# Recurrent memory attention, backward chain: output gradient by head in four column groups, 32-bit sums in column groups, LayerNorm input by DMA

## The chip, the cores and the metric

The kernel runs on one core of one Trainium2 chip. The metric is the device time of one execution in microseconds (us). Five instruction queues work side by side: TensorE (PE, with its weight loads shown as PEld), VectorE (DVE), ScalarE (ACT), GpSimd (POOL) and SyncE (SP), which only issues DMAs. SP and POOL issue the DMAs of the stage told here; 16 DMA engines carry them out.

## The reference

A layer of attention over segments with a recurrent memory, then a gated feed-forward layer, and the gradients of all of it. With S = 2048 rows, D = 448 columns, H = 16 heads of Dh = 256 (HD = 4096), M = 8 memory rows, segments of 32 rows (64 of them), so L = 40 rows per attention:

```python
mem = mem0
for s in range(n_seg):
    h = concatenate([mem, xs[s]])                     # 8 + 32 = 40 rows of 448
    q, k, v = h @ Wq, h @ Wk, h @ Wv                  # 16 heads of 256
    p = softmax(where(mask, q @ k.T / 16, -1e9))      # 40 x 40 per head
    o = (p @ v) @ Wo                                  # 40 rows of 448
    mem, out[s] = o[:8], o[8:]
h  = x + attention(layernorm(x))
h2 = h + (silu(layernorm(h) @ w_gate) * (layernorm(h) @ w_up)) @ w_down
return h2, vjp(grad_out)                              # h2 and nine gradients
```

Each segment takes its memory from the one before it; backwards, each segment's output gradient needs the memory gradient of the segment after it. So the 64 segments are a chain in both directions.

## The kernel before

The kernel has four stages, one after the other: the forward chain (to about 940 us of the span), the feed-forward layer with its gradients (to about 1257 us), the backward chain (`backward_chain`, to about 2253 us), and a tail with the weight gradients. The change lies in the backward chain and in the PSUM pools that it takes.

The loop of the backward chain runs over the segments s = 63 to 0, with `t, r = divmod(s, 4)`: four segments make a tile of 128 rows, and a tile is worked in the order r = 3, 2, 1, 0. The instructions within `with k.prio.crit()` go in the order in which they are written ahead of everything else; others fill the gaps as the scheduler places them. DMAs started with `nc.sync` stand in SP's queue in order, those with `nc.gpsimd` in POOL's. Each DMA of SP takes one of eight semaphores in turn and is issued when the DMA that had it before has landed.

What one segment does, with the lines of the kernel before:

- `prep_tile` (L1147, at r = 2 for the next tile) loads 128 rows of the output gradient from the DRAM tensor `DHb`, turned, as one transposing DMA of 128 x 512; POOL copies them into `do_roll` (L1150). `do_roll` holds, per segment, 40 columns: 0 to 31 are the segment's rows, 32 to 39 its memory rows, which the segment just worked has left there. The kernel keeps this order of the 40 rows throughout.
- `load_seg` (L1155 to L1168) loads the values turned (`load_v`, L1153, a transposing DMA), eight pieces of the queries and keys (L1163, runs of 2048 bytes, from the DRAM tensors T and T0) and, on POOL, the probabilities `P_sb` (L1166), which POOL copies to block-diagonal form (L1168).
- Output gradient: `WoT` as weights, `do_roll` as the moving side, 128 matmuls of 40 columns (L1236), so that each head's gradient comes out turned (`doT`); 16 transposes (L1245) give the same by rows (`dO_sb`).
- Score gradients: 32 matmuls (L1254), four DVE operations (L1261 to L1267) to `dS_bd`.
- `heads` (L1213): value, key and query gradients, 16 matmuls each; of the 40 rows, 0 to 7 (`first_rows`) go to `lo`, and 8 to 39 (`own_rows`) to `blk`. The turning of `dS_bd` is L1304.
- `rows_in` (L1293): 3 x 32 matmuls of 448 columns into one PSUM bank `pH`, four at a time in four column groups of 32, that is, four partial sums lie in the four groups of 32 partitions.
- `om` (L1319) copies `pH`; four fp32 matmuls with the matrix `sel` as moving side (L1322) add the four partial sums and turn them; the last eight of the 32 rows go to `do_roll` as the next segment's memory gradient (L1326), the other 24 are staged for the LayerNorm input `dxT`.
- Once per tile, outside the critical order and so filling gaps: the same products for the `lo` rows (L1378), their sums (L1385), four transposes of `dxT` (L1393), the LayerNorm gradient (`ln_bwd`, L253 to L264), and the stores.

All PSUM tiles come from three rotating pools: five banks `ps`, two `fx`, one `po`.

Of the kernel before, what the change touches and what calls it, by code (L numbers as in the profile page):

```python
# [9 lines left out]
FP32 = mybir.dt.float32  # L10
# [5 lines left out]
P = 128  # L16
# [129 lines left out]
def run_all(k: _K):  # L146
# [15 lines left out]
    psum = ctx.enter_context(tc.tile_pool(name="psum", bufs=1, space=bass.MemoryType.PSUM))  # L162
# [41 lines left out]
    def dt(name, shape, dtype=BF16):  # L204
# [7 lines left out]
              X_o=dt("X_o", [NB, P, MC * P]), HC=dt("HC", [NB * P, DP]), Oh=dt("Oh", [S, D]),  # L212
              DC0=dt("DC0", [P, 4, D]), DC1=dt("DC1", [P, NB - 4, D]))
# [18 lines left out]
    ffn_phase(k, lambda: next(back, None))  # L232
    for _ in back:
        pass
# [874 lines left out]
def backward_chain(k: _K):  # L1109
# [7 lines left out]
    NWIN = 8  # L1117

    WoT_sb = W(0, KC, HD)
# [4 lines left out]
    lo_b = {"v": [A(40, 32, 32), A(42, 32, 32)], "k": [A(44, 32, 32), A(46, 32, 32)], "q": [B(5, 32, 32)]}  # L1124
    dxT = B(7, 1024).bitcast(FP32).rearrange("p (c n) -> p c n", n=P)
    vT = A(49.5, 16, 2 * L)
    dO_sb = A(52, 16, P)
    doT = A(56, 32, 64)
    do_roll = A(60, KC, NWIN, L)
    xn_t = B(9, D)  # L1130
    dh_h = [B(9.875, 448).bitcast(FP32), A(48.5, 448).bitcast(FP32)]
    dx3 = A(48, KC * 48).bitcast(FP32).rearrange("p (c n) -> p c n", c=KC)
    lq3 = k.mv2[:].rearrange("p t n -> p (t n)").bitcast(BF16).rearrange("p (c m) -> p c m", m=M)
    dx2 = [(A(64.5, 96).bitcast(FP32).rearrange("p (c n) -> p c n", c=2), 0, 2, P, 2),
           (A(48.375, 48).bitcast(FP32).rearrange("p (c n) -> p c n", c=1), 2, 3, P, 2),
           (k.maskb[:, 0:24].unsqueeze(1), 3, 4, 64, 2)]
    dx1 = B(4.375, KC * 48).bitcast(FP32).rearrange("p (c n) -> p c n", c=KC)
    dx_stage = [(dx3, 0, KC, P, 3)] + dx2 + [(dx1, 0, KC, P, 1)]
    dhx = A(62.5, KC, P)
    dmr = A(63.5, KC, 16, M)  # L1140
    P_bd, dS_bd, dST_bd = [B(1.25 * i, 8, 2, L) for i in range(3)]
    Pb = [B(3.75, 8, L)]

    def prep_tile(t):
        if t < 0:
            return
        nc.sync.dma_start_transpose(out=dhx, in_=dr["DHb"][t * P:(t + 1) * P, :])  # L1147
        s0 = (4 * t) % NWIN
        for kc in range(KC):
            nc.gpsimd.tensor_copy(out=do_roll[:, kc, s0:s0 + 4, 0:SEG], in_=dhx[:, kc, :].rearrange("p (g j) -> p g j", g=4))  # L1150
# [4 lines left out]
    def load_seg(s):  # L1155
        if s < NSEG - 1:
            load_v(s)
# [488 lines left out]
```

## Time and profile before

Times of three runs: 2938.78 us median (2931.57 to 2948.37). The profiled execution took 2921.87 us.

| what | value |
|---|---|
| profiled execution, its span | 2921.87 us, 2920.1 us |
| clock granted to TensorE, mean | 0.995 |
| TensorE busy in 0 to 940, 940 to 1257, 1257 to 2253, 2253 to 2920 us | 873.6, 306.0, 979.0, 647.3 us |
| mean busy share of the DMA engines in the same four | 0.75, 0.93, 0.55, 0.81 |
| DVE, ACT, POOL busy in 1257 to 2253 us | 516, 380, 233 us |
| packets of the hardware queue, of the software queue | 692788, 49872 |

How to read it: a busy share is an average over stages, so the stages are taken apart by windows. A matmul's row gives start, length, line, what it writes and reads, and how many of the kind follow each other; lengths overlap a little, so costs are taken from start to start. "Waits" give who stood idle for what. A DMA's row on SP is the time of its issue; the transfer lands later, and the page counts what it moved in packets.

### The profile page before, as it was taken

The page shows a single profiled execution, that of the slowest core. Times are in us where ns is not written, and L with a number is a line of the kernel's source. Part 1 is how long each engine was busy: PE and PEld are TensorE (multiplying, and loading weights), DVE is VectorE, ACT ScalarE, POOL GpSimd, SP SyncE. Part 2 cuts the span into 40 slices and gives each one's busy share as a digit, 9 for nine tenths or more (in the row PEclk, how much of TensorE's full clock was granted, in tenths as well). Part 3 has the DMA queues.
Part 4 walks back from the last instruction along what each step waited for, and adds up shares of the span by engine and source line. Part 5 has one row for each costly group of instructions (what it writes and reads, how often), then busy time and mean ns, then how long its engine had stood idle before and what let it go on. Part 6 is the DMA issues. An engine that isn't in the chain of part 4 may idle for free.

```text
span 2920.1 us, 108265 instructions
## 1 busy us (share of the span) xinstructions
PE 2805.9 (96%) x47650; PEld 1746.3 (60%) x47650; DVE 1328.6 (45%) x3320; ACT 1077.0 (37%) x2590; POOL 704.1 (24%) x1676
## 2 busy tenths in 40 slices
PE   4999999999999999989999999999999989999998
PEld 3555565555555555667777777677766544545444
DVE  4555565556455666745555555555554011111110
ACT  2554454455454454433333333343333011111110
POOL 1222232233222222422222222222222111212211
PEclk9999999999999999999999999999999999999999
DMA  7577777777778988985555555555555998969941
GB/s 258 152 193 192 192 193 195 192 194 200 198 185 229 285 219 215 257 259 151 142 145 154 144 141 155 137 148 149 142 154 170 347 269 175 207 183 238 207 147 52
DMA packets 743132, 552.14 MB, mean 189 GB/s; under 512 B 601796, under 2 KB 639060, under 8 KB 740100
## 3 DMA queue, kind: packets, MB, share of 16 engines
q1 hardware_dynamic: 692788, 402.38, 55.9%
q0 software_dynamic: 49872, 142.83, 14.4%
q8 instruction: 374, 6.13, 0.9%
q14 instruction: 98, 0.80, 0.1%
HBM read 169.84 MB, written 236.13 MB: 139 GB/s over the span
## 4 chain that ended last, share of the span: by engine, by line
PE 80%; issue 8%; DMA 4%; ACT 3%; DVE 2%; POOL 2%; SPq 0%; POOLq 0%; ACTq 0%; DVEq 0%
PE po L1293 11%; PE psf L1487 8%; PE psf L1236 7%; PE psf L569 6%; PE psf L704 5%; PE psf L1213 5%; PE psf L967 4%; PE po L751 4%; PE fx L1378 3%; PE fx L1487 3%; PE fx L1091 3%; PE psf L593 2%; PE psf L1322 2%; PE psf L1245 2%; PE psf L485 2%
## 5 line engine op out<-in xcount | busy, mean ns | idle before, releaser
L76 ACT CAST arA<-psf 128x384 bf16<-128x384 f32 (+6 forms) x1083 | 419.8, 428 | 845.0 <-PE psf L1487 215.1
L75 DVE CAST arA<-psf 128x256 bf16<-128x256 f32 (+6 forms) x797 | 358.4, 471 | 687.8 <-PE psf L1487 248.9
L1293 PE MATMUL po<-arW,arA 128*32 128x448 bf16 x6144 | 328.1, 355 | 5.6 <-DMA arW<-Tq 4.1
L1487 PEld LDWEIGHTS <-arA 128*128 128x128 bf16 x1440 | 139.0, 98 | 160.6 <-issue 4.8
L1236 PEld LDWEIGHTS <-arW 128*128 128x128 bf16 x8192 | 211.2, 96 | 23.3 <-issue 18.4
L1487 PE MATMUL psf<-arW,arA 128*128 128x512 bf16 x882 | 222.7, 381 | 0.0
L1293 PEld LDWEIGHTS <-arA 128*32 128x32 bf16 x6144 | 146.8, 96 | 120.3 <-ACT arA L76 9.3
L1236 PE MATMUL psf<-arA,arW 128*128 128x40 bf16 x8192 | 217.2, 180 | 0.8 <-DVE arA L1326 0.8
L704 PE MATMUL psf<-arW,arA 128*64 128x512 bf16 x1536 | 212.1, 382 | 0.0
L569 PE MATMUL psf<-arW,arA 128*32 128x512 bf16 x3072 | 189.8, 381 | 7.7 <-DVE arA L75 0.9
L76 ACT COPY arA<-psf 128x512 bf16<-128x512 bf16 (+3 forms) x206 | 142.9, 727 | 39.5 <-PE psf L593 24.0
L76 ACT CAST arB<-psf 128x64 bf16<-128x64 f32 (+1 forms) x320 | 107.7, 337 | 135.1 <-PE psf L576 73.6
L967 PE MATMUL psf<-arW 128*128 128x256 bf16 (+1 forms) x1288 | 149.0, 277 | 5.0 <-DVE arA L75 3.7
L75 DVE COPY arA<-psf 128x512 bf16<-128x512 bf16 (+2 forms) x204 | 104.3, 512 | 99.5 <-PE psf L1245 82.4
L967 PEld LDWEIGHTS <-arW 128*128 128x128 bf16 (+1 forms) x1344 | 103.2, 97 | 56.9 <-issue 45.4
L569 PEld LDWEIGHTS <-arA 128*32 128x32 bf16 x3072 | 70.3, 96 | 105.1 <-issue 28.8
L751 PE MATMUL po<-arW,arA 128*32 128x256 bf16 (+1 forms) x4096 | 126.9, 261 | 1.2 <-DVE arA L75 1.2
L1564 POOL DMA_DIRECT2D out_dram<-arA x96 | 52.2, 544 | 262.0 <-DVE arA L75 233.6
L1527 PE MATMUL psf<-arW 128*128 128x448 bf16 x525 | 111.6, 352 | 3.0 <-DVE arA L75 1.6
L1213 PEld LDWEIGHTS <-arW 128*128 128x128 bf16 x2048 | 79.5, 99 | 49.6 <-issue 48.1
L751 PEld LDWEIGHTS <-arA 128*32 128x32 bf16 x4096 | 104.0, 96 | 8.5 <-DVE arA L75 1.5
L1168 POOL COPY arB<-arB 40x320 bf16<-40x320 bf16 x128 | 58.9, 460 | 174.8 <-DMA arB<-P_all 86.7
(298 smaller groups left out, 4553.5 us busy)
## 6 DMA issues: line engine op xcount, KB each, us to landing
arW<-T SPq DMA_DIRECT2D x256, 128.0 KB
X_o<-arA SPq DMA_DIRECT2D x37, 512.0 KB
T<-arA SPq DMA_DIRECT2D x64, 256.0 KB
X_v<-arA POOLq DMA_DIRECT2D x30, 512.0 KB, 4.9
X_k<-arA POOLq DMA_DIRECT2D x30, 512.0 KB, 4.7
X_q<-arA POOLq DMA_DIRECT2D x30, 512.0 KB, 4.1
out_dram<-arA POOLq DMA_DIRECT2D x84, 128.0 KB, 3.8
VG<-arA SPq DMA_DIRECT2D x64, 160.0 KB
```

The lines of the kernel that those rows point to most:

```text
L75: return nc.vector.tensor_copy(out=out, in_=in_)
L76: return nc.scalar.copy(out=out, in_=in_)
L569: nc.tensor.matmul(banks[b][w][32 * q:32 * q + 32, :], lhsT=hT_roll[:, kc, sl, M:L], rhs=(Wq_sb, Wk_sb)[w][:, kc, col(q, b)], start=(b == ...
L704: nc.tensor.matmul(pV[b][64 * g:64 * g + 64, 0:512], lhsT=hT_flat[:, kc, sl * L:sl * L + 64], rhs=Wv_sb[:, kc, n * 512:(n + 1) * 512], sta ...
L751: last = nc.tensor.matmul(pO[32 * q:32 * q + 32, 0:w], lhsT=xblk[:, j, r * SEG:(r + 1) * SEG], rhs=Wo_sb[:, cj(j), 256 * dh:256 * dh + w], ...
L967: nc.tensor.matmul(ps[fp][:, f2 * 256:(f2 + 1) * 256], lhsT=Wt[lo:hi, kc, c * P:(c + 1) * P], rhs=xT[lo:hi, kc, :], start=(kc == 0 and f2 ...
L1091: k.last_dh = nc.tensor.matmul(pdh[:, 0:D], lhsT=srcT[:, tt, c, :], rhs=WT[:, c, :], start=(i == 0), stop=(i == 2 * FC - 1))
L1213: nc.tensor.matmul(ps[b][:, i * 2 * L:(i + 1) * 2 * L], lhsT=lhs[:, at, :], rhs=rhs_bd[:, cl // 2, :, :].rearrange("p g n -> p (g n)"), st ...
L1236: nc.tensor.matmul(pss[b][:, jj * L:(jj + 1) * L], lhsT=WoT_sb[:, kc, c * P:(c + 1) * P], rhs=do_roll[:, kc, sl, :], start=(kc == 0), stop ...
L1293: nc.tensor.matmul(pH[32 * (j % 4):32 * (j % 4) + 32, 0:D], lhsT=blk[nm][:, j, r * SEG:(r + 1) * SEG], rhs=WT[:, cj(j), :], start=(nm == " ...
L1487: k.last_mm = nc.tensor.matmul(pa[i][:, 0:w], lhsT=lhs_of(b)[:, i // 2 * P:(i // 2 + 1) * P], rhs=rhs_of(q, b, i % 2), start=(b == 0), sto ...
L1527: k.last_mm = nc.tensor.matmul(pa[i][:, 0:D], lhsT=lhs_of(b, i), rhs=rhs_of(b), start=(bi == 0), stop=(bi == m + 3))
```

## The change

The diff touches `backward_chain` and the PSUM pools:

- PSUM: after the feed-forward stage the three pools are closed, and eight banks are named one by one (`k.bank(i)`).
- Output gradient (`grads_by_col`): now columns 8 to 39 of `do_roll` (the "own" rows) are the weights and `WoT` the moving side, 512 columns wide, in four column groups (one per group of heads): 32 matmuls instead of 128. D = 448 is held as four chunks of 112. Eight transposes (`grads_turned`) give the turned form. Rows 0 to 7 (the "rest", which need no other segment) are done for the four segments of a tile at once (`hRo`), one tile ahead, at the ends of r = 2 and r = 1; they are saved to DRAM (`RO`) and loaded again by rows (`load_rest`).
- Value gradients: `value_rest` and `value_own`, 8 + 8 matmuls of 160 columns, with probabilities loaded by twelve small DMAs (`load_p`).
- Sums: `summed` has `sel` as weights, and adds the four partial sums by four fp32 matmuls of 112 columns, in column groups; the result is cast (`ot`), turned by one transpose and copied to `do_roll`.
- LayerNorm input: the summed rows go to DRAM (`DXQ` per segment, `DXR` per tile) and are loaded as a tile of 128 x 448 (`norm_load`); `norm_first` and `norm_second` replace `ln_bwd` here, two tiles later. The products of the `lo` rows are issued by hand (`rest_parts`) in numbers per segment.
- `prep_tile` is called at r = 3 and loads 112-column chunks of `DHb`, four transposing calls of 128 x 112. In the order of the built program the four stand as plain copies with a pattern 112 x 128 x 1, where the one of before stands as a transpose.

The loads of a segment stand in SP's queue in the order `load_rest`, `load_p`, `load_v`, `load_qk`, DXQ, DXR, norm loads (r = 2), `prep_tile` (r = 3).

```diff
+    k.bank = bank
+    k.ps1 = lambda: turns("ps", 0, 5, "psf")
+    k.fx1 = lambda: turns("fx", 5, 2, "fx")
+    k.po1 = lambda: bank(7, "po")
+    k.ph1 = lambda: psum2.tile([P, 1024], BF16, tag="bank7", name="ph", bufs=1)
...
     def prep_tile(t):
         if t < 0:
             return
-        nc.sync.dma_start_transpose(out=dhx, in_=dr["DHb"][t * P:(t + 1) * P, :])
+        for c in range(4):
+            nc.sync.dma_start_transpose(out=dhx[0:DQ, c, :], in_=dr["DHb"][t * P:(t + 1) * P, DQ * c:DQ * c + DQ])
         s0 = (4 * t) % NWIN
-        for kc in range(KC):
-            nc.gpsimd.tensor_copy(out=do_roll[:, kc, s0:s0 + 4, 0:SEG], in_=dhx[:, kc, :].rearrange("p (g j) -> p g j", g=4))
+        for c in range(4):
+            nc.gpsimd.tensor_copy(out=do_roll[0:DQ, c, s0:s0 + 4, 0:SEG], in_=dhx[0:DQ, c, :].rearrange("p (g j) -> p g j", g=4))
+        nc.gpsimd.tensor_copy(out=hRo[0:DQ].rearrange("p k (g j) -> p k g j", j=M), in_=do_roll[0:DQ, :, s0:s0 + 4, 0:M])
+
+    def grads_by_col(lhs, bank, b, c0=0, c1=4):
+        for c in range(c0, c1):
+            for q in range(4):
+                n0 = 1024 * q + 512 * b
+                last = nc.tensor.matmul(bank[32 * q:32 * q + 32, :], lhsT=lhs(c), rhs=WoT_sb[0:DQ, c, n0:n0 + 512],
+                                        start=(c == 0), stop=(c == 3), skip_group_check=True)
+        return last
+
+    def rest_lhs(c):
+        return hRo[0:DQ, c, :]
+
+    def grads_turned(bank, src, dst, b, eng="v"):
+        pt = bank[:].bitcast(BF16)
+        for i in range(4):
+            last = nc.tensor.transpose(pt[:, i * P:(i + 1) * P], src[:, i * P:(i + 1) * P], ident[:, :])
+        return last, k.evac(dst.rearrange("p (x c) n -> p x c n", x=2)[:, :, 8 * b:8 * b + 8, :],
+                            pt[:, 0:512].rearrange("p (c x n) -> p x c n", x=2, n=32), eng)
+
+    def rest_saved(t, b, src):
+        nc.sync.dma_start(out=dr["RO"][t][:, 512 * b:512 * b + 512], in_=src)
+
+    def load_rest(s):
+        t, r = divmod(s, 4)
+        src = dr["RO"][t].rearrange("(q r k) n -> r q k n", q=4, k=M)
+        for w, a, m, n in ((0, 0, 0, 3), (1, 0, 3, 3), (0, 3, 6, 2)):
+            nc.sync.dma_start(out=dOr[32 * w:32 * w + 32, a:a + n].rearrange("p m e -> p (m e)"), in_=src[r][:, :, P * m:P * (m + n)])
+
+    def load_p(s):
+        pa = dr["P_all"][s].rearrange("p (x i n) -> p x i n", x=2, n=L)
+        for q in range(4):
+            g, x = divmod(q, 2)
+            for w in range(2):
+                p0 = 32 * w + M * q
+                nc.sync.dma_start(out=P4r[p0:p0 + M, 2 * x + g], in_=pa[64 * g:64 * g + M, x])
+            nc.sync.dma_start(out=P4[32 * q:32 * q + 32, 2 * x + g], in_=pa[64 * g + M:64 * g + L, x])
...
+    def value_rest(ps):
+        for m in (0, 3, 1, 4, 2, 5, 6, 7):
+            w, a = divmod(m, 3) if m < 6 else (0, m - 3)
+            last = nc.tensor.matmul(v_out(ps, m), lhsT=dOr[32 * w:32 * w + 32, a, :], rhs=p_rows(P4r[32 * w:32 * w + 32], m),
+                                    start=m in (0, 3, 6), stop=False, skip_group_check=True)
+        return last
+
+    def value_own(ps, m0, m1):
+        for m in range(m0, m1):
+            last = nc.tensor.matmul(v_out(ps, m), lhsT=dO_own[:, m * P:(m + 1) * P], rhs=p_rows(P4, m),
+                                    start=False, stop=True, skip_group_check=True)
+        return last
...
+    def summed(ps, part):
+        for q in range(4):
+            last = nc.tensor.matmul(ps[32 * q:32 * q + 32, 0:DQ], lhsT=sel[:], rhs=part[:, DQ * q:DQ * q + DQ],
+                                    start=True, stop=True, skip_group_check=True)
+        return last
...
+    def rest_out():
+        summed(pX, om2)
+        nc.scalar.copy(out=pxs, in_=pX[:, 0:DQ])
...
+    def norm_load(t):
+        x = norm[t] = [om2, None]
+        own = dr["DXQ"][4 * t:4 * t + 4].rearrange("r (q n) d -> r n q d", q=4)
+        rest = dr["DXR"][t].rearrange("(q r n) d -> r n q d", q=4, n=M)
+        for r in range(4):
+            x4 = x[0][:].rearrange("p (q d) -> p q d", q=4)
+            nc.sync.dma_start(out=x4[32 * r + M:32 * r + 32], in_=own[r, 0:24])
+            nc.sync.dma_start(out=x4[32 * r:32 * r + M], in_=rest[r])
+        rows = slice(t * P, (t + 1) * P)
+        nc.sync.dma_start(out=xn_t, in_=dr["XN"][rows, 0:D])
+        for c0 in (0, 224):
+            nc.sync.dma_start(out=dh_h[c0 // 224], in_=dr["DH"][rows, c0:c0 + 224])
+
+    def norm_first(t):
+        x, rstd, junk = norm[t][0], k.rstd1[:, t:t + 1], k.bank(3)
+        m1, m2 = [smal.tile([P, 1], FP32, name=f"lnb_m{i}") for i in (1, 2)]
+        nc.scalar.activation(out=x[:], in_=x[:], func=ACT.Copy, accum_out=m1[:])
+        nc.vector.tensor_tensor_reduce(out=junk[:, 0:D], in0=x[:], in1=xn_t, scale=1.0, scalar=0.0,
+                                       op0=ALU.mult, op1=ALU.add, accum_out=m2[:])
+        m1s, m2s = [smal.tile([P, 1], FP32, name=f"lnb_m{i}s") for i in (1, 2)]
+        nc.vector.tensor_scalar(out=m1s[:], in0=m1[:], scalar1=-1.0 / D, scalar2=rstd, op0=ALU.mult, op1=ALU.mult)
+        nc.vector.tensor_scalar(out=m2s[:], in0=m2[:], scalar1=-1.0 / D, scalar2=None, op0=ALU.mult)
+        nc.vector.scalar_tensor_tensor(out=x[:], in0=xn_t, scalar=m2s[:], in1=x[:], op0=ALU.mult, op1=ALU.add)
+        norm[t][1] = m1s
+    def norm_second(t):
+        x, m1s = norm.pop(t)
+        nc.scalar.activation(out=x[:], in_=x[:], func=ACT.Identity, scale=k.rstd1[:, t:t + 1], bias=m1s[:])
+        for c0 in (0, 224):
+            nc.vector.tensor_tensor(out=xn_t[:, c0:c0 + 224], in0=x[:, c0:c0 + 224], in1=dh_h[c0 // 224], op=ALU.add)
+        nc.gpsimd.dma_start(out=OUT1[t * P:(t + 1) * P, :], in_=xn_t)
+
+    V_FILL = {3: 16, 2: 18, 1: 17, 0: 3 * MC}
...
-        if r == 2:
+        if s < NSEG - 1:
+            load_rest(s)
+            load_p(s)
+            load_v(s)
+            load_qk(s)
+            nc.sync.dma_start(out=dr["DXQ"][s + 1], in_=dxs)
+            if r == 3 and t + 2 < NT:
+                nc.sync.dma_start(out=dr["DXR"][t + 2], in_=pxs)
+            if r == 2 and t + 2 < NT:
+                norm_load(t + 2)
+        if r == 3:
             prep_tile(t - 1)
-        if s < NSEG - 1:
-            load_seg(s)
 
         with k.prio.crit():
-            pss = [k.ps1() for _ in range(4)]
...
-                        nc.tensor.matmul(pss[b][:, jj * L:(jj + 1) * L], lhsT=WoT_sb[:, kc, c * P:(c + 1) * P],
-                                         rhs=do_roll[:, kc, sl, :], start=(kc == 0), stop=(kc == KC - 1))
...
-                    nc.tensor.transpose(ph[:, i * P:(i + 1) * P], doT[:, c0:c0 + 2, :].rearrange("p c n -> p (c n)"), ident[:, :])
...
+            own = [k.bank(0), k.bank(1)]
+            for b in range(2):
+                with tc.issue_after(k.last_dh.ins) if s == NSEG - 1 and b == 0 else nullcontext():
+                    grads_by_col(lambda c: do_roll[0:DQ, c, sl, M:L], own[b], b)
+            for b in range(2):
+                k.evac(dO_own[:, 512 * b:512 * b + 512], own[b][:], "vs"[b])
+            nc.gpsimd.tensor_copy(out=doT[:, :, 0:M], in_=R4_b[t % 2][:, :, r * M:(r + 1) * M])
+            pV = [k.bank(2 + b) for b in range(3)]
+            value_rest(pV)
+            grads_turned(k.bank(0), dO_own[:, 0:512], doT[:, :, M:L], 0)
+            value_own(pV, 0, 4)
+            last_t, turned_v = grads_turned(k.bank(1), dO_own[:, 512:], doT[:, :, M:L], 1)
+
...
+            if r in (0, 1) and t > 0:
+                with tc.issue_after(last_d.ins):
+                    last_t, _ = grads_turned(k.bank(0), rO, R4_b[(t - 1) % 2], 1 - r)
+                rest_saved(t - 1, 1 - r, rO)
...
+            with tc.issue_after(last_v.ins):
+                rest_parts(V_FILL[r])
...
-            k.last_om = nc.vector.tensor_copy(out=om[:, 0:D], in_=pH[:, 0:D])
-            pm = k.ps1()
-            for kc in range(KC):
-                nc.tensor.matmul(pm[:, kc * 32:(kc + 1) * 32], lhsT=om[:, kc * P:(kc + 1) * P], rhs=sel[:],
-                                 start=True, stop=True)
-            pm3 = pm[:, 0:KC * 32].rearrange("p (c m) -> p c m", m=32)
...
+            nc.vector.tensor_copy(out=om[:, 0:2 * DQ], in_=pH[:, 0:2 * DQ])
+            nc.scalar.copy(out=om[:, 2 * DQ:D], in_=pH[:, 2 * DQ:D])
+            with tc.issue_after(last_r.ins):
+                if r in (2, 1) and t > 0:
+                    pR = pD
+                    last_r = grads_by_col(rest_lhs, pR, 2 - r)
+                elif parts:
+                    last_r = rest_parts(14)
+            pq = k.bank(2)
+            with tc.issue_after(last_r.ins):
+                summed(pq, om)
+            nc.vector.tensor_copy(out=ot, in_=pq[:, 0:DQ])
             if s > 0:
-                nc.vector.tensor_copy(out=do_roll[:, :, (s - 1) % NWIN, SEG:L], in_=pm3[:, :, 24:32])
+                pm = k.bank(3)[:].bitcast(BF16)
+                nc.tensor.transpose(pm[0:DQ, 0:P], ot, ident[:, :])
+                nc.vector.tensor_copy(out=do_roll[0:DQ, :, (s - 1) % NWIN, SEG:L],
+                                      in_=pm[0:DQ, 0:P].rearrange("p (c n) -> p c n", n=32)[:, :, 24:32])
...
+            nc.scalar.copy(out=dxs, in_=pq[:, 0:DQ])
+            if r in (2, 1) and t > 0:
+                k.evac(rO, pR[:], "s")
+            if r in (2, 1) and t + 2 < NT:
+                with tc.issue_after(cast["v"].ins):
+                    (norm_first if r == 2 else norm_second)(t + 2)
...
-            px = k.fx1()
...
-            ln_bwd(k, halves, pX[:, 0:D], xn_t, k.rstd1[:, t:t + 1], t1[:], t1[:])
...
+    nc.sync.dma_start(out=dr["DXQ"][0], in_=dxs)
+    for t in (1, 0):
+        if t == 0:
+            rest_parts(len(parts))
+            nc.scalar.copy(out=om2[:], in_=pX[:, 0:D])
+            rest_out()
+        nc.sync.dma_start(out=dr["DXR"][t], in_=pxs)
+        norm_load(t)
+        norm_first(t)
+        norm_second(t)
```

## The prediction

> **What bounds the kernel now.** I read the page first (engines), then stretches of the span, then TensorE in time order over one segment, then the queue that feeds it.
>
> ```profile
> span 2920.1 us, 108265 instructions
> PE 2805.9 (96%) x47650; PEld 1746.3 (60%) x47650; DVE 1328.6 (45%) x3320; ACT 1077.0 (37%) x2590; POOL 704.1 (24%) x1676
> q1 hardware_dynamic: 692788, 402.38, 55.9%
> ```
>
> TensorE is busy 96% of the span, so I ask whether that holds in the backward chain, the only stage that the diff touches. Stretches, each with us, busy time by engine, granted clock, DMA share:
>
> ```profile
> 1297.00:2237.00 940.00, 931.53 (x22561) 673.93 (x22557) 490.70 (x1195) 361.11 (x1030) 221.03 (x552) 1.00 0.53 145
> 1700.00:1761.90 61.90, 61.40 (x1489) 44.37 (x1486) 32.40 (x80) 23.86 (x68) 15.58 (x36) 1.00 0.53 149
> ...
> 2404.00:2408.00 4.00, 0.99 (x9) 0.96 (x9) 1.02 (x2) 1.04 (x1) 0.74 (x1) 0.50 1.03 383
> 2408.00:2412.00 4.00, 4.00 (x13) 1.44 (x11) 0.43 (x1) 1.96 (x2) 0.76 (x2) 0.58 1.03 402
> 2412.00:2416.00 4.00, 4.00 (x32) 2.27 (x31) 0.69 (x1) 0.06 (x1) 0.00 (x0) 1.00 1.01 361
> ```
>
> The chain is TensorE end to end: 931.5 of 940 us. One tile of four segments repeats every 61.86 us (14.88 for r = 2, 1, 0; 17.2 for r = 3). The last three rows, from the tail, show the one long wait of the trace (8.2 us): afterwards the clock stays near half for some 4 us, a loss of about 2 us. One segment on TensorE (start, us, line, out<-in, count):
>
> ```profile
> 1711.94 3.37 PE L1236 MATMUL psf<-arA,arW 128*128 128x40 bf16 x128
> 1715.15 1.12 PE L1245 MATMUL psf<-ident,arA 128*128 128x128 bf16 x16
> 1716.20 0.69 PE L1254 MATMUL psf<-arA 128*64 128x40 bf16 x32
> 1716.92 0.75 PE L1213 MATMUL psf<-arB,arA 128*128 128x80 bf16 x16
> ...
> 1717.87 1.70 PE L1293 MATMUL po<-arW,arA 128*32 128x448 bf16 x32
> ...
> 1721.94 2.64 PE L1293 MATMUL po<-arW,arA 128*32 128x448 bf16 x52
> ...
> 1725.32 1.08 PE L1322 MATMUL psf<-sel,omb 128*128 128x32 f32 x8
> 1726.33 0.56 PE L1378 MATMUL fx<-arW,arA 128*32 128x448 bf16 x7
> 1726.82 3.37 PE L1236 MATMUL psf<-arA,arW 128*128 128x40 bf16 x128
> ```
>
> Starts follow without a gap, so every us taken off TensorE is won, as long as nothing else becomes late. What could be late are the loads on SP's queue. The row loads of one tile's output gradient (one transposing DMA per tile), who waits for them, and one value-gradient transpose with the packets of its window 1699.7 to 1704:
>
> ```profile
> L1147 SPq DMA_TRANSPOSE arA<-DHb x16: 1189/1224/2437, 1227.2 to 2057.8; - x16
>   POOL arA L1150: 3.7, 2
> q1 hardware_dynamic: 1312, 0.33, 36.3%
> arA<-VG SPq DMA_TRANSPOSE x1
> ```
>
> Today that load costs 1.2 us of issue, lands 2.6 to 7.4 us later (median 5.2), and cost POOL 3.7 us in the whole run. Nearly all 1312 packets are the transpose's 256-byte ones: 0.363 x 16 x 4300 ns / 1312 = 19 ns each.
>
> **The change, part by part** (us per tile; TensorE rows from start to start).
>
> *1. Removed on TensorE.* Output gradient L1236 4 x 3.21, turning L1245 4 x 1.05, value heads (a third of L1213) 4 x 0.67, fp32 sums L1322 4 x 1.01, L1385 1.17, LayerNorm turning L1393 1.06 with its wait: 26.0.
>
> *2. Added on TensorE.* The own rows are 32 column-group matmuls of 512 columns; the forward's L569 (24 in 1.41 us, 0.216 per group of four) gives 8 x 0.216 + 0.115 = 1.84. Eight turns by L593 (four in 0.233) 0.47. Value gradients: 16 of 160 columns by L666, 0.068 each, 1.09. The first rows once per tile: 1.84 + 0.47. The four fp32 `summed` matmuls with 112 columns have no row. Ends: 0.3 (a column group of bf16 with 448 columns takes 0.19, L1293) and 1.0 (today's eight fp32 records); I take 0.5, between, since their columns are 112 wide as against 32; five a tile make 2.5, with 0.24 for the turns of `ot`. Sum 18.7.
>
> *3. New waits on TensorE.* A hop over DVE or ACT costs the operation + 0.18 (0.30 behind fp32). Scores wait about 0.3 for the turned gradient's copies (0.41). After `summed`: cast 0.19 + 0.30, turn, copy 0.19 + 0.18, some 0.95, where today seven products of L1378 cover L1326. 4 x 1.25 = 5.0. The copies of `om` (0.33 by halves) and of `own` (0.69, 0.59) are hidden by the fillers of L1506 or the rest gradients, and by `value_rest` and the second bank; uncovered they would add 0.5 and 0.6 a segment.
>
> *4. LayerNorm.* Its chain (rows L253 to L262: ACT 0.55, DVE 0.62, 0.20, 0.14, 0.68, ACT 0.76, together 2.95) now stands, in r = 1, ahead of the copies of the value gradients in ACT's order, and `rows_in` on TensorE waits behind those. Ends 0 and 2.95; I take 2.0, as the score matmuls (0.72) hide some. Costing it at nothing would need its inputs to land a segment earlier.
>
> If each remaining row kept its gap, the tile were 61.86 - 26.0 + 18.7 + 7.0 = 61.6. Walking the four segments by rows, with the longer runs of L1293 at 0.19 per group (as in its 52), I get 13.7 + 13.95 + 16.4 + 14.2 = 58.25 for r = 3, 2, 1, 0. I take the walk, as it carries each wait, and keep 61.6 as the other end.
>
> *5. SP's queue.* Per segment 25 DMAs instead of 9 (`load_rest` 3, `load_p` 12, `load_v` 1, `load_qk` 8, DXQ 1); per tile 11 norm loads, 2 RO, DXR, 4 of `prep_tile`: 118. At 0.37 (median) to 0.48 (mean) from start to start and 1.34 for a VG transpose, 47.5 to 60 us of issue. That still fits into 58 to 62 by a little.
>
> *6. `prep_tile`.* One transposing DMA of 128 x 512 becomes four of 128 x 112. In the order of the built program these stand no longer as transposes but as plain copies 112 x 128 x 1 (VG's remain transposes): each reads runs of one element, two bytes. 4 x 112 x 128 = 57,344 runs, 3,584 for each of 16 engines. The trace writes one packet per contiguous run. No run of two bytes is in it; the nearest rows are its packet records: 4 bytes 9 ns (median; mean 13), 128 bytes 11, 160 bytes 14, 256 bytes 18, while the VG packets follow each other every 20.8 ns. Ends: 20.8 ns, and below, 4.6 (the line through 256 and 128 bytes meets zero at 4 ns; 4 x 20.8/18). I take 9 x 20.8/18 = 10.4 ns: 37.3 us. The software queue's share of the engines here (180 of 930 us) slows that by 0 to 9 us, I take 4; issue and landing 2.5. So E = 43.8 us after r = 3 begins.
>
> Who waits: the four stand on SP ahead of every load of r = 2, in order, and eight semaphores taken in turn let only seven more loads be issued before the last of the four lands. POOL's copies of the loaded rows (L1168 and L1169 after the change) wait too, and behind them POOL's load of `P_sb` and its copies for r = 2 (ready by E + 7, before the T loads). After E: eight P loads, VG and eight T loads are issued (17 starts, 9.4), the last lands 3.6 later (today's T loads), then q heads 0.67, 64 row products 3.0 (the k heads have run), rest gradients 0.92, `summed` 0.5 and the hops 0.95: r = 2 ends at E + 19.1. For r = 1 SP has 11 norm loads ahead of 15 rest and P loads: issued at E + 22.6, landed 2 later, where `value_rest` wants them at 21.0; its T loads are late by another 1, and LayerNorm counts in part: 19.6. r = 0: 14.2. Tile = E + 52.9 = 96.7, or +34.8. Fifteen tiles load a next one: +523.
>
> The Trainium skill, "DMA: Bandwidth & Descriptors", "Rules for kernel authors", puts a plain DMA with a rearranged access pattern at a 19-fold difference to the transpose, which speaks against this step. By it, on today's landing of 2.6 us (least) and 5.2 us (median), an estimate is 49 to 99 us in place of 43.8; on the packets' own time alone (448 packets, some 0.6 us) it were 11. The same page ("Constraints") says that inputs with a free dimension below 128 can fall back to such a pattern; 112 is below. The trace has no such load, so the run decides.
>
> *7. Once.* The first `prep_tile` stands ahead of weight loads Tk, To, Tv, Tq in a stretch with DMA share 0.98 (1237 to 1297): 0 to 44, I take 20. TensorE waits some 38 us per tile, so the half clock of the 2404 rows: 2 x 15 = 30 (0 to 30). The last tile has no load: -3.6. At the end 17 DMAs stand ahead of the tail's first loads: +4.
>
> **Sum:** 2921.9 + 523 - 3.6 + 20 + 30 + 4 = 3495, against the profiled execution (span 2920.1). The median shown, 2938.8, is 0.6% above that; I say 3500.
>
> **The rivals.**
> - *A, the load is hidden: faster.* Place: SP's queue in r = 3. If a two-byte run costs under 2 ns per engine, then E is below 9.0 (61.86 - 52.9) and the tile gains. Fully hidden, 16 x (58.25 - 61.86) + 4 gives 2868 (to 2920 by the 61.6). For: the transpose itself is cheap today. Against: no packet in the trace is that short, 9 ns at 4 bytes.
> - *B, dearer:* if two-byte runs cost more than 20.8 ns, E is above 81 and the time above 4077.
> - *C, issue on SP:* if the load is hidden (below 2 ns) but every issue takes the mean 0.48, and SP also stands 0.85 per segment for `dxs`, a tile takes 60.1 + 3.4 = 63.5: 2921.9 + 16 x 1.64 + 4 = 2952. For: 118 DMAs; against: the median of 0.37.
> - *D, between,* 2 to 4.6 ns: 2950 to 3075.
>
> **How the numbers follow.** Chances: my case 0.80 (4.6 to 20.8 ns, with the ends of step 7: 3075 to 4077), B 0.04, A 0.09, C 0.04, D 0.03. About 0.5% (15 us) is what a measurement of this kernel can tell from no change. A gives faster 0.08 and same 0.01, a C milder than worked out same 0.01; all else is slower, 0.90. The range, 3100 (5 ns) to 4100, leaves out A, B, C and D, 0.20. The likeliest case stands at 3500.
>
> **What would show it.** In the profile after: segment periods in the backward chain in the order some 14, 49, 20, 14 us (r = 3, 2, 1, 0) instead of 17, 15, 15, 15; TensorE waits once a tile, named after DMA loads of P or T, or POOL's `doT`; L1165 as plain copies with 57,344 packets of 2 bytes a tile, and the packet count of q1 up by some 900,000; granted clock below 1 after each wait; own gradient near 1.84 a segment and `summed` 0.3 to 1.0. Wrong it would be if L1165 lands within 9 us, if loads behind it land before it, or if the r = 2 wait is short while SP is never idle (C).

## The result and the profile after

The changed kernel takes 3914.32 us (median of 4 runs, 3898.79 to 3926.31), the kernel before 2935.65 us in the same comparison: a ratio of 1.3321 with a 95% interval of 1.325 to 1.3392. The profiled execution has a span of 3921.5 us, 1001 us above that of before. The page:

```profile
span 3921.5 us, 98059 instructions
PE 2821.7 (72%) x41631; PEld 1622.5 (41%) x41631; DVE 1329.1 (34%) x3415; ACT 1033.3 (26%) x2510; POOL 714.3 (18%) x1659
q1 hardware_dynamic: 1656116, 422.68, 69.0%
PE 51%; DMA 29%; SPq 7%; issue 6%; ACT 3%; DVE 2%; POOL 1%; POOLq 0%; ACTq 0%; DVEq 0%
L1298 PE MATMUL bank<-arA 32*128 32x160 bf16 x512 | 62.9, 273 | 845.0 <-DMA arA<-P_all 791.6
```

TensorE's busy time has hardly moved (2806 to 2822 us, part of it now at a lower clock), while its share fell from 96% to 72%. The hardware queue carries 963,000 packets more; the chain that ended last has 29% of DMA in it. One group, the first matmuls of `value_rest` (L1298), stands behind 845 us of idle time, 792 of it ended by the loads of probabilities (`load_p`, the P loads below).

Where the 1001 us lie can be read from the first and the last turn of a segment's sums: in before from the starts of L1236 (1281.05 and 2237.55 us), in after from those of L1513 (1404.81 and 3216.42 us), both the end of s = 63 and of s = 1.

| part | before | after | difference |
|---|---|---|---|
| to the end of s = 63 | 1281.1 | 1404.8 | +123.8 |
| s = 62 to s = 1 | 956.5 | 1811.6 | +855.1 |
| from there to the end | 682.6 | 705.1 | +22.5 |

One tile of after in TensorE's order (start, us, line, out<-in, count, and in brackets the idle time before and what ended it):

```profile
2075.70 1.90 PE L1175 MATMUL bank<-arW,arA 112*32 112x512 bf16 x30 [0.70 <-issue]
2125.05 0.84 PE L1298 MATMUL bank<-arA 32*128 32x160 bf16 x8 [47.45 <-DMA arA<-P_all]
...
2138.47 0.26 PE L1513 MATMUL bank<-ident,identf 128*112 128x128 bf16 x1 [0.38 <-DVE identf L1510]
...
2147.52 0.95 PE L1298 MATMUL bank<-arA 32*128 32x160 bf16 x8 [5.46 <-DMA arA<-P_all]
...
2150.54 0.57 PE L1416 MATMUL bank<-arA 128*64 128x40 bf16 x12 [1.36 <-DMA arA<-VG]
```

In r = 2 the own gradient is ready at 2077.6, then TensorE stands 47 us for the P loads; in r = 1 it stands again, 5.5 us for P and 1.4 for VG. The same tile on SP's queue (start, time of the issue, line):

```profile
2062.35 40.85 SPq L1165 DMA_DIRECT2D arA<-DHb  x3
2103.29 14.23 SPq L1196 DMA_DIRECT2D arA<-RO  x3
2117.58 0.80 SPq L1204 DMA_DIRECT2D arA<-P_all  x2
...
2123.37 1.34 SPq L1208 DMA_TRANSPOSE arA<-VG  x1
...
2128.01 0.33 SPq L1216 DMA_DIRECT2D arW<-T0k  x1
```

Three of the four row loads hold SP for 41 us, the next three loads for another 14 (the first of them for 12.9); only then does SP go on at some 0.3 to 1.3 us per DMA. All of the row loads, who waited for them, and the queues in the window 2065 to 2115:

```profile
L1165 SPq DMA_DIRECT2D arA<-DHb x64: 313/13022/15751, 1232.1 to 3080.7; - x64
  POOL arA L1168: 773.6, 64
...
q1 hardware_dynamic: 54655, 0.11, 119.2%
...
arA<-DHb SPq DMA_DIRECT2D x3, 28.0 KB
arB<-P_all POOLq DMA_DIRECT2D x1, 80.0 KB, 7.5
```

So the loads are no longer transposes. 54,655 packets move 0.11 MB: two bytes each. In the packet records they come in 16 bursts of 57,344, each 52.8 to 59.6 us long (15.3 ns per packet and engine in the median burst), together 917,504. A DMA of POOL's queue is slowed to 7.5 us (before: 3.2) but goes through in the middle of the burst, while what stands behind the row loads in SP's own queue waits for its end.

Stretches around the wait (us, busy time by engine, granted clock, DMA share, GB/s):

```profile
2080.00:2120.00 40.00, 0.00 (x0) 0.00 (x0) 0.00 (x0) 0.00 (x0) 0.88 (x3) 0.52 1.34 4
2124.00:2129.00 5.00, 3.95 (x56) 3.38 (x56) 1.12 (x3) 0.62 (x2) 0.24 (x1) 0.50 0.74 176
2129.00:2134.00 5.00, 5.00 (x113) 3.04 (x115) 3.74 (x10) 2.52 (x9) 2.09 (x5) 0.96 0.44 109
```

The granted clock is 0.50 in the first 4 us after TensorE has work again, and 0.96 in the 5 us after that.

### The profile page after: what moved, and what is told of

It reads as the page before. It is cut to its first block, busy times and chain, and to the rows that moved or that the text cites. A ratio compares the mean times of both kernels' runs of the same rounds, so it can differ in the third digit from the quotient of the medians.

```text
span 3921.5 us, 98059 instructions
## 1 busy us (share of the span) xinstructions
PE 2821.7 (72%) x41631; PEld 1622.5 (41%) x41631; DVE 1329.1 (34%) x3415; ACT 1033.3 (26%) x2510; POOL 714.3 (18%) x1659
## 4 chain that ended last, share of the span: by engine, by line
PE 51%; DMA 29%; SPq 7%; issue 6%; ACT 3%; DVE 2%; POOL 1%; POOLq 0%; ACTq 0%; DVEq 0%
DMA arA<-DHb 21%; PE psf L1649 6%; PE bank L1316 6%; PE psf L587 4%; PE psf L722 4%; PE po L769 3%; SPq L1165 3%; PE bank L1175 3%; PE psf L985 2%; PE fx L1649 2%; PE psf L611 2%; SPq L1204 2%; DMA arA<-VG 2%; PE bank L1416 1%; PE fx L1109 1%
## 5 line engine op out<-in xcount | busy, mean ns | idle before, releaser
L1298 PE MATMUL bank<-arA 32*128 32x160 bf16 x512 | 62.9, 273 | 845.0 <-DMA arA<-P_all 791.6
L76 ACT CAST arA<-bank 128x96 bf16<-128x96 f32 (+4 forms) x606 | 192.4, 376 | 910.1 <-PE bank L1304 891.3
L1298 PEld LDWEIGHTS <-arA 32*128 32x128 bf16 x512 | 34.0, 104 | 880.1 <-issue 801.3
L1316 PE MATMUL bank<-arW,arA 128*32 128x448 bf16 x6144 | 346.3, 378 | 1.4 <-issue 1.4
L75 DVE COPY arA<-bank 128x512 bf16<-128x512 bf16 x143 | 60.8, 425 | 825.9 <-PE bank L1185 823.1
L75 DVE CAST arA<-psf 128x512 bf16<-128x512 f32 (+2 forms) x285 | 160.1, 562 | 504.4 <-PE psf L1649 249.9
L76 ACT CAST arA<-psf 128x512 bf16<-128x512 f32 (+3 forms) x379 | 190.1, 510 | 534.7 <-PE psf L1649 215.1
L1168 POOL COPY arA<-arA 112x128 bf16<-112x128 bf16 x64 | 18.9, 295 | 773.6 <-DMA arA<-DHb 773.6
L75 DVE CAST arA<-bank 128x384 bf16<-128x384 f32 (+4 forms) x385 | 131.3, 392 | 69.7 <-PE bank L1175 54.3
L1175 PE MATMUL bank<-arW,arA 112*32 112x512 bf16 x2048 | 132.3, 401 | 10.0 <-DVE arA L1514 7.5
L1689 PE MATMUL psf<-arW 128*128 128x448 bf16 x525 | 117.5, 364 | 16.4 <-DMA arW<-X_o 10.2
```

The lines of the kernel that those rows point to most:

```text
L75: return nc.vector.tensor_copy(out=out, in_=in_)
L76: return nc.scalar.copy(out=out, in_=in_)
L1175: last = nc.tensor.matmul(bank[32 * q:32 * q + 32, :], lhsT=lhs(c), rhs=WoT_sb[0:DQ, c, n0:n0 + 512], start=(c == 0), stop=(c == 3), skip_ ...
L1298: last = nc.tensor.matmul(v_out(ps, m), lhsT=dOr[32 * w:32 * w + 32, a, :], rhs=p_rows(P4r[32 * w:32 * w + 32], m), start=m in (0, 3, 6), ...
L1316: last = nc.tensor.matmul(ps[32 * q:32 * q + 32, 0:D], lhsT=lhs(j), rhs=WT[:, cj(j), :], start=(start and i < 4), stop=(stop and i >= len( ...
L1689: k.last_mm = nc.tensor.matmul(pa[i][:, 0:D], lhsT=lhs_of(b, i), rhs=rhs_of(b), start=(bi == 0), stop=(bi == m + 3))
```

## The experiments

Three theories were on record. Theory 1: the two-byte runs are the whole loss. Theory 2: the many DMAs on SP's queue are too many by themselves, by their order (2a) or by the sum of their issue times (2b). Theory 3: the column groups and their new waits cost TensorE more than they save.

### The row loads as transposes again

```diff
-            nc.sync.dma_start_transpose(out=dhx[0:DQ, c, :], in_=dr["DHb"][t * P:(t + 1) * P, DQ * c:DQ * c + DQ])
+            nc.sync.dma_start_transpose(out=dhx[:, c, :], in_=dr["DHb"][t * P:(t + 1) * P, DQ * c:DQ * c + P])
```

> The changed kernel with one edit: the four row loads of prep_tile take 128 columns instead of 112, so that each stands as a transpose in the built program; nothing else differs. Theory 1 (the two-byte runs are the whole loss, the rest of the change gains): a tile takes 58 to 62 us as worked out without them, 2870 to 2920 us in all. Theory 2 (118 DMAs per tile on SP are too many by themselves): the loss stays in part, a tile takes 64 to 75 us, 2960 to 3140 us. Theory 3 (column groups with their new waits cost TensorE more than they save): a tile takes 62 to 66 us with SP idle in between, 2930 to 2990 us.

Measured: 3158.12 us (3148.37 to 3163.76), ratio 1.0741 (1.0691 to 1.0792). This edit alone takes 756 of the 979 us back. But a quarter of the loss stays: theory 1 is not the whole, and theory 2 lies nearest (3158 is a little above its range). A tile (from the end of one r = 3 to the next) takes 72 to 81 us from the third on; the first two, which have no norm loads yet, take 63 and 60. One tile, SP's queue:

```profile
1808.46 5.82 SPq L1165 DMA_TRANSPOSE arA<-DHb  x4
...
1830.12 0.30 SPq L1351 DMA_DIRECT2D om<-DXQ  x1
1837.71 0.34 SPq L1190 DMA_DIRECT2D RO<-arA  x1
...
1841.17 2.07 SPq L1196 DMA_DIRECT2D arA<-RO  x3
...
1847.68 1.36 SPq L1208 DMA_TRANSPOSE arA<-VG  x1
```

The four transposes still hold SP for 5.8 us, ahead of the loads of r = 2, which takes 16 to 22 us instead of 14. Then SP stands from 1830.4 to 1837.7 at the write to RO, whose data ACT makes only at the end of r = 2, and behind it stand the rest of the norm loads and the 15 rest and P loads of r = 1. TensorE and its clock then:

```profile
1848.14 0.84 PE L1298 MATMUL bank<-arA 32*128 32x160 bf16 x8 [6.73 <-DMA arA<-P_all]
...
1851.32 0.57 PE L1416 MATMUL bank<-arA 128*64 128x40 bf16 x12 [1.70 <-DMA arA<-VG]
...
1853.77 3.18 PE L1316 MATMUL bank<-arW,arA 128*32 128x448 bf16 x32
```

The 32 row products take 3.18 us instead of 1.70: half clock again (0.52 granted in 1853 to 1858). So r = 1 takes 24 to 27 us, while r = 0 and r = 3 run at 14.7 and 14.0 in most tiles.

### The runs added to the kernel before

```diff
+        for c in range(KC):
+            nc.sync.dma_start_transpose(out=dhx[0:112, c, :], in_=dr["DHb"][t * P:(t + 1) * P, 112 * c:112 * c + 112])
         nc.sync.dma_start_transpose(out=dhx, in_=dr["DHb"][t * P:(t + 1) * P, :])
```

> The kernel before with one addition: ahead of its transposing load of the rows (which overwrites them) stand the four plain copies of 112 x 128 two-byte runs of the changed kernel. Theory 1: SP is held for some 41 us and its ring for 55 us per tile, of which a few us are hidden: +45 to +60 us per tile for 15 tiles, 3600 to 3850 us. Theories 2 and 3: the copies cost little here, below 3200 us.

Measured: 3738.25 us (one run), +805 us over the kernel before (2933.61), within the range of theory 1. TensorE's work is untouched here; one addition to one queue does it. SP's queue in one tile:

```profile
2027.50 44.46 SPq L1148 DMA_DIRECT2D arA<-DHb  x4
2072.05 13.06 SPq L1165 DMA_DIRECT2D arW<-T  x1
2085.16 0.32 SPq L1165 DMA_DIRECT2D arW<-T0q  x1
```

### Half the dose

```diff
+            n = DQ if c < 2 else P
+            nc.sync.dma_start_transpose(out=dhx[0:n, c, :], in_=dr["DHb"][t * P:(t + 1) * P, DQ * c:DQ * c + n])
```

> The changed kernel with two of the four row loads as transposes of 128 columns and two as before, plain copies of two-byte runs: half the dose. Theory 1: the drain of a tile falls from 55 to 28 us, the wait with it: 3914 - 15 x 27.5 = 3500, with the clock back earlier 3450 to 3530 us. Theory 2 or 3: less than 150 us are won, above 3760 us.

Measured: 3514.26 us (one run), within the range of theory 1. With 4, 2 and 0 of the four loads as runs the kernel takes 3914, 3514 and 3158 us: 400 us for the one half, 356 for the other. The bursts here have 28,672 packets and last 27 to 31 us. These three points lie nearly on a straight line: half the runs cost about half the time.

### RO written on ACT's queue

From the first experiment's kernel:

```diff
-        nc.sync.dma_start(out=dr["RO"][t][:, 512 * b:512 * b + 512], in_=src)
+        nc.scalar.dma_start(out=dr["RO"][t][:, 512 * b:512 * b + 512], in_=src)
```

> The kernel of e1_transposed (3158 us) with one edit: the two writes of the rest gradients to RO per tile go out on ACT's queue instead of SP's. Theory 2a (order: SP stands 7.3 us at this write until ACT has made its data, with the norm loads and the 15 rest and P loads of r = 1 behind it): r = 1 falls from 25 to 27 us to 17 to 19, about 8 us in each of 13 tiles, 3040 to 3070 us. Theory 2b (rate: the sum of some 60 us of issue per tile is what binds SP): 0.7 us per tile are freed, 3140 to 3160 us.

Measured: 3107.71 us (one run), 50 us less: between the two. r = 1 fell by 2 to 4 us, not by 8, since the 11 norm loads still stand ahead of its own. The standing at one write is part of it; what else stands ahead of those loads is the subject of the next edit.

### The norm traffic off SP

```diff
-            nc.sync.dma_start(out=dr["DXQ"][s + 1], in_=dxs)
+            nc.scalar.dma_start(out=dr["DXQ"][s + 1], in_=dxs)
```

The same for DXR; in `norm_load` all eleven `nc.sync` become `nc.gpsimd`.

> The kernel of e4_ro_on_act with two more edits: DXQ and DXR are written on ACT's queue, the 11 norm loads per tile go out on POOL's. SP keeps 25 - 1 DMAs per segment and the four transposes of prep_tile. Theory 2a: only 1 to 3 us per tile more are won than by the edit before, 3000 to 3050 us. Theory 2b: SP's issue falls from 60 to some 53 us per tile, the tile to 62 to 64 us, 2930 to 2970 us. Theory 3 (TensorE work or its new waits bind): no more than by e4.

Measured: 3020.19 us (3017.62 to 3036.62), ratio 1.0288 (1.0262 to 1.0315), 88 us less than the edit before. r = 1 is down to 14.7 us; r = 3 takes 16 to 21 and r = 2 after it some 16. The first products of r = 2 stand ahead of the last turn of r = 3 in TensorE's order, and their P loads stand behind the four transposes on SP's queue:

```profile
1697.67 5.59 SPq L1165 DMA_TRANSPOSE arA<-DHb  x4
...
1710.42 0.42 PE L1298 MATMUL bank<-arA 32*128 32x160 bf16 x2 [4.40 <-DMA arA<-P_all]
```

Neither theory is confirmed as it stood. The time lies in the range of theory 2a, but the gain of some 6 us per tile is more than its 1 to 3; the tile stays at 62 to 72 us and the time 50 us above the range of theory 2b, for the transposes were not in its sum as an obstacle to other loads. The eleven norm loads also stood ahead of the loads of r = 1, so this edit changes both order and number, and does not tell the two apart.

### One transposing DMA per tile

`DHb` is written in four chunks of 112 columns with a pitch of 128, so that 128 x 512 can be loaded by one DMA; the readers of `DHb` for the weight gradients follow.

```diff
-        for c in range(4):
-            nc.sync.dma_start_transpose(out=dhx[:, c, :], in_=dr["DHb"][t * P:(t + 1) * P, DQ * c:DQ * c + P])
+        nc.sync.dma_start_transpose(out=dhx, in_=dr["DHb"][t * P:(t + 1) * P, :])
...
-            nc.scalar.copy(out=dh_b[:, 0:D], in_=dh_t)
+            nc.scalar.copy(out=dh_b.rearrange("p (c n) -> p c n", c=4)[:, :, 0:D // 4], in_=dh_t.rearrange("p (c n) -> p c n", c=4))
```

> The kernel of e5_norm_off_sp with one more edit: DHb is written in four chunks of 112 columns with a pitch of 128, so that one transposing DMA of 128 x 512 loads a tile's rows (1.2 us of issue instead of 5.8). Theories 2a and 2b: r = 2 falls from some 18.6 to 14 us, the tile to 58 to 60 us, 2870 to 2910 us. Theory 3: the tile stays at 61.9 us or above, 2930 us or more.

Measured: 2954.92 us (2949.43 to 2975.34), ratio 1.0083 (1.0051 to 1.0115). Most tiles take 57 to 61 us, about as expected and below the 61.86 of before: theory 3 falls for the chain. But the time is 45 us above the expected range. Every fourth tile takes 66 us (its memory rows are turned by four DMAs, 6.0 us on SP), and the start and the end of the chain are longer than before's.

### Memory rows, start and end

```diff
-            for c in range(4):
-                nc.sync.dma_start_transpose(out=rows[:, DQ * c:DQ * c + DQ], in_=dmr[0:DQ, c].rearrange("p s m -> p (s m)"))
+            nc.sync.dma_start_transpose(out=rows[:, 0:D].rearrange("p (c n) -> p c n", c=4), in_=dmr[0:DQ].rearrange("p c s m -> p (c s m)"))
...
-    load_p(NSEG - 1)
+    load_p(NSEG - 1, nc.scalar)
```

Also on ACT's queue: the first `load_rest`, and at the end OUT2, DXQ and DXR.

> The kernel of e6_one_transpose (2955 us) with three more edits: the memory rows of every fourth tile are turned by one transposing DMA instead of four (6.0 us of SP, behind which a segment waited 4 to 7 us and the clock fell); the first segment's P and rest loads go out on ACT's queue (there SP stood 10.2 us behind the large weight loads, TensorE 9.2 us); at the end OUT2, DXQ and DXR are written on ACT's queue, so that SP reaches the tail's X_o loads sooner. Theory 2b (what is left is SP's queue): 4 x 8 us + some 8 us at the start + 0 to 8 at the end, 2900 to 2920 us, below the kernel before (2935). Theory 3 (the column-group stage gains nothing by itself and 2955 is its level): 2940 to 2960 us.

Measured: 2937.27 us (2925.45 to 2951.75, 12 runs), ratio 1.0011 (0.9991 to 1.0031): no difference from the kernel before that can be told, and between the two ranges expected (2900 to 2920, 2940 to 2960). No tile takes more than 63.5 us now, and the stretch of the table above, s = 62 to s = 1, takes 921.6 us, 34.9 less than before. The start takes 29.3 us more and the end 16.3 us more. At the start, on TensorE:

```profile
1288.14 0.61 PE L1187 MATMUL bank<-ident,om 128*128 128x128 bf16 x4 [19.92 <-ACT om L76]
...
1300.01 3.18 PE L1318 MATMUL bank<-arW,arA 128*32 128x448 bf16 x32
```

ACT's copy into `om` waits 22.5 us until the feed-forward stage's last gradient, which lies in the same buffer, has been stored. One and the same stretch of the chain, first in the kernel before:

```profile
1330.00:2200.00 870.00, 863.39 (x20896) 624.22 (x20892) 455.43 (x1108) 335.71 (x956) 204.71 (x508) 1.00 0.53 145
```

The changed kernel:

```profile
1330.00:2200.00 870.00, 440.88 (x7933) 261.12 (x7933) 229.44 (x599) 148.75 (x447) 105.48 (x247) 0.74 0.80 83
```

This one:

```profile
1330.00:2200.00 870.00, 816.00 (x16172) 491.10 (x16168) 471.36 (x1234) 303.98 (x918) 310.54 (x670) 0.99 0.65 171
```

TensorE is busy 99%, 51% and 94% of it. Freed of most waits for loads, the new scheme needs less TensorE time per tile, and still leaves it idle for 54 us of 870, where before it left 7.

### Three tries to win the start and the rest

```diff
-            dh_t = k.f32(("f3", "f1")[tt], (D, DP)[tt], "dh_t")[:, 0:D]
+            dh_t = k.f32(("f1", "f3")[tt], (DP, D)[tt], "dh_t")[:, 0:D]
...
+                with tc.issue_after(pool_op.ins):
+                    norm_load(t + 2)
```

> The kernel of e7_memory_and_ends (2937 us, tiles at 60 us instead of 61.9, the first segment ending at 1310 us where the kernel before ends it at 1281) with two edits at the start of the chain: the last two tiles of the feed-forward stage use their two buffers in the other order, so that the buffer which the chain's first output gradient needs is stored first (TensorE waited 19.9 us for that store), and the norm loads on POOL may not stand ahead of that store. If the lost gain sits at the start: the wait falls to 5 to 10 us, 2920 to 2928 us. If the store only comes late because the weight loads fill the DMA engines: no change, 2932 to 2940 us.

Measured: 2959.79 us (2955.67 to 2969.03), ratio 1.0098 (1.0077 to 1.0118). A miss: TensorE's waits for the turned gradients at the start became 15 us instead of 22, but the last feed-forward tile ends 6 us later, and the norm loads are now held back in every tile. ACT stands 42.3 us at LayerNorm's first operation until they have landed (9.8 in e7_memory_and_ends), and its copies of `om` keep TensorE waiting (waits in the window 1500 to 2200: total, times, longest):

```profile
PE bank L1324 <- ACT om L1503: 18.2, 11, 4.9
```

The same wait in the kernel of e7_memory_and_ends:

```profile
PE bank L1324 <- ACT om L1502: 0.2, 1, 0.2
```

The next moves the three `load_rest` of every segment to ACT's queue:

```diff
-            load_rest(s)
+            load_rest(s, nc.scalar)
```

> The kernel of e8_start with one more edit: the three load_rest DMAs of each segment (2.0 us of SP) go out on ACT's queue. If SP's queue is still what makes r = 0 and r = 1 longer than 14.0 and 14.7 us: 1 to 2 us per tile are won, 15 to 30 us less than e8_start. If ACT then stands at them until the rows are free, with the copies for TensorE behind: slower than e8_start by 10 us or more.

Measured: 2976.4 us (2972.11 to 2987.03), 17 us more than e8_start: the second branch. TensorE waits for ACT's copies of the own gradient as well (17.6 us in 11 waits in the same window). The last puts the four P4 loads of each segment, in the kernel of e7_memory_and_ends, on POOL's queue:

```diff
-            eng.dma_start(out=P4[32 * q:32 * q + 32, 2 * x + g], in_=pa[64 * g + M:64 * g + L, x])
+            (nc.gpsimd if eng is nc.sync else eng).dma_start(out=P4[32 * q:32 * q + 32, 2 * x + g], in_=pa[64 * g + M:64 * g + L, x])
```

> The kernel of e7_memory_and_ends (2937 us) with one more edit: the four P4 loads of each segment (32 x 160, 1.3 us of SP) go out on POOL's queue. If SP's queue is what is left of the chain's delay (r = 1 and r = 0 at 15 to 17 us over a floor of 14.6 and 13.9): 1 to 1.5 us per tile, 2912 to 2925 us, below the kernel before. If POOL's four issues of 0.54 us ahead of its load of P_sb make that late instead: the same or slower, 2935 to 2970 us.

Measured: 2972.73 us (2966.55 to 2985.22), ratio 1.0132 (1.0094 to 1.0169): slower, a little above the range of the second branch. r = 1 and r = 0 are at 14.7 and 14.6 us in most tiles now, but r = 3 takes 15 to 25 us. Waits in the same window:

```profile
PE bank L1318 <- ACT arA L76: 30.2, 8, 8.9
...
ACT om L1363 <- DMA om<-DXR: 38.3, 7, 10.3
```

The second line in the kernel of e7_memory_and_ends:

```profile
ACT om L1363 <- DMA om<-DXR: 9.8, 4, 5.1
```

POOL's wait for `P_sb` is at most 7.4 us, 3.9 before this edit: what the second branch named. But TensorE waits for copies on ACT, up to 8.9 us at a time, and ACT is late because of LayerNorm's first operation (L1363), which stands ahead of these copies until the norm loads have landed: each of TensorE's nine waits of over 2.5 us in the chain ends 1.1 us after ACT has begun that operation. The norm loads stand on POOL's queue, to which this edit adds the P4 loads; that these delay them is likely, and was not tested. In all three tries this wait of ACT grew, from 9.8 us to 42.3, 42.2 (with the first try's edits in it) and 38.3: a queue that had time to spare lost it at one operation that stood for its data.

### The runs with the norm traffic off SP

The kernel of e5_norm_off_sp with the four loads of 112 columns back.

> The kernel of e5_norm_off_sp (3020 us) with the four row loads of prep_tile back as in the changed kernel, 112 columns and so plain copies of two-byte runs; RO, DXQ, DXR and the norm loads stay off SP's queue. If the two causes add up: 3914 - (3158 - 3020) = 3776 us. If the order of SP's queue costs more because it starts behind a late r = 2 (r = 1 took 23 to 24 us in the changed kernel, 25 to 27 in e1_transposed): 3640 to 3740 us. If the long wait hides it: 3880 us or more.

Measured: 3793.07 us (one run); with the sum of both effects 3776 was expected. r = 1 had taken 25 to 27 us in the changed kernel too, so the second branch had no ground. The two causes add up to within 17 us: 773 us for the runs here against 756 with the norm traffic on SP, and 121 us for that traffic here against 138.

## Why the prediction was right, and where it was not

**The direction and its cause (step 6)** hold. The four loads are plain copies, 57,344 packets of two bytes a tile and 917,504 in all (about 900,000 were named); TensorE waits long once a tile for P loads, POOL for the rows themselves; the edit that only gives the transposes back wins 756 us. Rival A, the hidden load, needed less than 2 ns per run; measured are 15.3 ns. Rival B (above 20.8 ns) is excluded by the same number.

**The size of that step is the term that was too small.** E was put at 43.8 us: 37.3 for the drain (the time of a burst) at 10.4 ns, 4 for sharing, 2.5 besides. The drain, sharing included, took 52.8 to 59.6 us. The single packet was well guessed (median 9 ns, as the row of 4-byte packets), the bursts were not: their mean is 16.8 ns, a tenth of them takes 33 ns or more. That is +14 us per tile (55 for 41.3). The upper end of that step, 20.8 ns, had been kept in the range.

**What the step did not see: SP itself is held.** The working let seven more loads be issued during the drain and left eight P loads for after it. In fact each of these loads after the first holds SP for 12 to 16 us, and the next DMA behind them for 11 to 13; in the tile shown all 12 P loads were issued after the drain, and TensorE starts 7.7 us after its end. r = 2 took 62 to 72 us instead of 49 (between ends of segments, from the second tile on).

**r = 1** was put at 19.6 us with the norm loads ahead of its own, the right mechanism; 25 to 27 were measured from the third tile on, the first with norm loads. What was missing is the write to RO between them, at which SP stood until its data were there (from 2132.7 to 2138.4 in the tile shown, 7.3 us in that of e1_transposed), and the half clock after the second wait. Step 5 counted issue times and said that they fit "by a little"; the first experiment shows that the queue does not keep up: +14 us per tile without any runs. A sum of issue times says nothing of a queue that stands at one DMA for its data.

**The start** was put at +20 with an end of 44. Measured +124, for two loads fall before the end of s = 63: the weights To came behind the first (TensorE waits 40.5 us for it), and the P loads of s = 62 behind the second; the first products that need these stand ahead of the last turn of s = 63 (51 us). The second had been counted among the fifteen; the working put only one at the start. **The clock** (2 us a tile) is right in kind: 0.50 for 4 us after the long wait shown. **The end** was put at +4 and took 22.5; with its writes off SP (e7_memory_and_ends) 16 remain, and what makes them stays open.

The terms against the profiled executions: 1001 us = 124 + 855 + 22. The forecast 3495 made 573 of it, 523 of these from the tiles that load a next one, TensorE's gain taken off; the runs alone were measured at 756 to 805. Without them the profiled execution of e1_transposed is still 241 us behind: 186 in s = 62 to s = 1, which are gone in e7_memory_and_ends, after DMAs were moved off SP's queue and transposes joined, 36 at the start and 19 at the end. For SP's order and number of DMAs the sum had little, some 3 us a tile in r = 1, as rival C held them to be cheap (2952). So the gain on TensorE was right, and both costs, the runs and the queue, were too low. That 3914 still lies in the range is in part luck: the upper end of 20.8 ns left room for costs that were not in the sum.

**Steps 1 to 4** come out well. The own gradient takes 1.84 us a segment from start to start, as worked out from L569; `summed` 0.56 (0.3 to 1.0, taken 0.5); without waits r = 3, 2, 1, 0 take 13.9, 14.1, 14.7, 14.6 us in e7_memory_and_ends, where 13.7, 13.95, 16.4 and 14.2 were walked. LayerNorm's +2.0 in r = 1 did not show there. The tile of 58.25 is near what most tiles of e6_one_transpose take (57 to 61), in part by luck: without waits the four make 57.3, and waits elsewhere fill the rest. So the change does on TensorE what it is meant to do, 2 to 4 us per tile, and loses it on the queue of its loads, and in e7_memory_and_ends at the start and the end.

The Trainium skill, "DMA: Bandwidth & Descriptors", "Rules for kernel authors", has a rearranged access pattern at a 19-fold difference to the transpose; of the prediction's estimates by it the one on today's landing, 49 to 99 us, holds the 55 us measured, the one on the packets' own time (11 us) does not. The same section says that spreading DMAs over SP, ACT and GpSimd does not help bandwidth and saves only issue time. Bandwidth was not what was short here (the DMA engines' share was 0.51 in the chain of e1_transposed), and the spreading brought 138 us; but 50 of these came with two writes to RO per tile, whose issue takes 0.34 us each: what was saved there is time in which SP stood for data.

## What to carry to other kernels

Look in the built program at what a transposing load has become before counting it: chunks of 112 columns instead of 128 turned four loads that hold their queue for 5.8 us into four that hold it for 55. A queue in order is to be walked like an engine: what it issues, what it waits for at each DMA, and who stands behind; the sum of the issue times is only its lower bound. And in a stage that is 99% busy on its engine, a saving of 6% there (58.25 us for 61.86) is worth only what the queue that feeds it lets through.

## What was not expected of the hardware

- The issue of a DMA is not always short: the first of four loads with 14,336 runs took 0.3 to 0.6 us of SP, each further one 12 to 16, and the next DMA behind them 11 to 13 (12 to 15 in e2_before_plus_runs, where it is a load of T or VG). That their queue had no more room is a likely reading, which no run tests.
- Packets of two bytes took a median of 9 ns like those of 4 bytes, but a burst of them moved on at 15.3 ns per packet and engine, and four of these loads moved 115 KB in 55 us.
- A DMA of the other queue passed through such a burst in 7.5 us (3.2 without).
